# Reordering a causal linear attention with a top-2 mixture of experts behind it: low parts inside routing steps, q ahead of v, gathers moved up, gates read later, zeros written in other places

## The chip, the cores and the metric

One core of one Trainium2 chip runs the whole kernel. The metric is device time in microseconds of one execution, as the median of several runs. The profile is one further execution, and all rows below are from it.

## What is computed

The attention is a linear one with a decay per head: a state of 64 x 64 per head is decayed and added to at every step, and y is q times the state. Its output, 3072 tokens of 512 numbers, is x for the experts. Each token goes to the two of eight experts with the largest noisy logits.

```python
# q, k, v: (4, 8, 768, 64)
for t in range(S):
    state = gamma[None, :, None, None] * state + np.einsum('bhd,bhe->bhde', k[:, :, t], v[:, :, t])
    y[:, :, t] = scale * np.einsum('bhd,bhde->bhe', q[:, :, t], state)
x = y.transpose(0, 2, 1, 3).reshape(3072, 512)
logits = x @ w_gate
noisy_logits = logits + np.log1p(np.exp(x @ w_noise)) * noise
top2 = np.argpartition(-noisy_logits, 2, axis=1)[:, :2]
...
for e in range(8):
    for k in range(2):
        mask = top2[:, k] == e
        h = np.maximum(x[mask] @ w1[e], 0.0)      # 512 -> 1024
        out[mask] += top2_w[mask, k, None] * (h @ w2[e])
```

## The kernel before

Nothing is ordered by a scheduler: the order in which the Python code calls the helpers is the order of each engine's instructions, and tile pools add the waits. The kernel has three parts.

**The loop over 24 chunks** (4 batches of 6 chunks of 128 tokens, from 10 to 118.6 us). Chunk j of the loop runs, in this order: `qk(j+1)` on TensorE (q times k), `v_scale(j+1)` and `q_scale(j+2)` on GpSimd (decay tables into v and q, lines 339 and 345), the loads of chunk j+4 on SyncE's queue, `masked(j+1)` on VectorE (line 373), `x_store(j-3)`, `y_in(j)` on TensorE (line 379), then `x_total`, `x_hi` of chunk j-1 (sum of squares, power of two, high half of x in fp16 by ScalarE), then what the table `between` holds for chunk j, `y_mm(j)`, `x_rows(j-2)` (transposes), `logits(j-2)`, then what `todo` holds, then `slip()`, then what `late` holds. `slip()` runs `x_lo` of chunk j-1 on VectorE (line 417): the low half of x, what the fp16 high half leaves over. It is the last reader of that chunk's y in PSUM; there are two such buffers, so `y_in(j)` waits for `x_lo(j-2)`.

Routing of a batch is spread over the following chunks. With n the last chunk of batch b: `route_a` late in n+2 (logits, softplus), `route_b` between n+3 (top two: six `max`, six `max_index`), `route_b2` and `route_c` between n+4 (one-hot rows, `den` = second minus first logit at line 493, and three small rows `cb`), `places` on TensorE and `route_d` in n+5, `route_e` in n+6 and n+7 (one-hot tables), `route_w` in n+8 (gate weights, written to `gbuf`), `table` on TensorE at the end of n+8, `route_f` between n+9 (adds the table to `acc`). For the second batch, `rows_of` follows there (lines 596 to 599: row numbers `idx` for the gathers), then at the end of that chunk, 20, three indirect gathers `xg<-xbuf,idx` on GpSimd's queue (line 684), and in chunks 21 and 22 three DMA transposes `xe<-xg` on SyncE's queue (line 706): the input of the first expert. In chunks 11 to 19 GpSimd also makes the halves of the first expert's w1 (`wst`, `w1l`, lines 227 and 231).

SyncE's queue also carries the zeros that `out` starts from (the experts add into it): `zero_out(i)`, line 305, at the end of chunks 12, 14, 16, 18, 20 and 21, each two pieces of 512 KB in rows of 1 KB (one for either half of the columns), and in chunk 22 two of 128 KB.

**Between the loop and the second expert** (to about 195 us) TensorE runs the first expert for the batches that are routed, in small units (`early`: `mm1` for a first product, `mm2` for a second), between the last batch's routing steps. `mm1(0, SECOND, CAPS[0], n)`, n from 0 to 7, is the first expert's third part; in it stand `out_scale(0, mid, NBLK)` (gates of the rows, lines 952 to 961, from gathers `gx`) at n = 5 and, from n = 4, `x_sums(1)`: sums and differences of the second expert's transposed input on VectorE (lines 845 to 852), each with a ScalarE step `xt` (line 853).

**Experts 1 to 7** (`mm1s`, a Strassen-like first product of 30 slots, each six matmuls, with a `hook` after every slot; then `mm2`). At slot 11 the hook runs `out_scale(e, ...)`, which waits for the gathered gates `gx`.

## Time and profile before

| | us |
|---|---|
| median of 3 runs | 642.06 |
| lowest, highest of them | 640.72, 649.16 |
| the profiled execution | 644.05 |
| its span from first to last instruction | 642.3 |
| TensorE busy | 615.4 |
| VectorE busy | 451.6 |
| ScalarE busy | 392.3 |
| GpSimd busy | 394.0 |

The profile calls the engines PE (TensorE), PEld (its weight loads), DVE (VectorE), ACT (ScalarE), POOL (GpSimd) and SP (SyncE); SPq is SyncE's queue, which issues DMAs. A row of a timeline starts with the start in us from the span's start and the duration in us; in square brackets stands how long the engine was idle before it and what ended that. In a row of waits, the engine and its line stand left of the arrow, the one waited for right of it. A window's row gives each engine's busy time and number of instructions, then the granted TensorE clock, the busy share of the DMA engines and GB/s. Busy time of an engine says little on its own: a wait of TensorE moves the end, an idle VectorE does not.

### The profile page before, as it was taken

What the parts mean: (1) busy time and instruction counts of PE and PEld (TensorE: products, weight loads), DVE (VectorE), ACT (ScalarE), POOL (GpSimd) and SP (SyncE); (2) the same over time, 40 slices, a digit from 0 to 9 for tenths busy, and PEclk for the clock granted to TensorE, in tenths of its full rate; (3) what the DMA queues carried; (4) which work ended last, traced back from release to release, by engine and by line L of the source; (5) the groups of instructions that cost most, each with busy time, mean ns of one, the idle gap of its engine ahead of it and who ended that gap; (6) DMA issues with size and microseconds to landing.
All of it is one profiled execution on the core that took longest, in us unless ns stands there. A gap on an engine that the chain in (4) does not pass through costs nothing.

```text
span 642.3 us, 13225 instructions
## 1 busy us (share of the span) xinstructions
PE 615.4 (96%) x5133; PEld 387.0 (60%) x5133; DVE 451.6 (70%) x947; ACT 392.3 (61%) x655; POOL 394.0 (61%) x279
## 2 busy tenths in 40 slices
PE   8999988899989899999999999999999999999995
PEld 5898877656756444654465446544654465445784
DVE  4668999577768599179917991799279747957730
ACT  4688878763447656486648664866476558656311
POOL 3455998244477847882688457744883676484164
PEclk9999999999999899999999999999999999999998
DMA  8999999953966499459644974597469746942043
GB/s 307 340 391 404 383 381 336 289 193 103 179 105 166 77 155 308 53 110 206 211 52 82 205 243 52 93 194 245 51 103 193 230 48 112 243 53 33 7 53 44
DMA packets 107393, 112.90 MB, mean 176 GB/s; under 512 B 64512, under 2 KB 84224, under 8 KB 103744
## 3 DMA queue, kind: packets, MB, share of 16 engines
q1 hardware_dynamic: 86080, 84.29, 45.2%
q0 software_dynamic: 20528, 26.90, 27.1%
q8 instruction: 41, 0.67, 0.4%
q10 hardware_dynamic: 720, 0.84, 0.4%
q14 instruction: 24, 0.20, 0.1%
HBM read 72.16 MB, written 26.47 MB: 154 GB/s over the span
## 4 chain that ended last, share of the span: by engine, by line
PE 71%; DVE 11%; DMA 10%; ACT 3%; POOL 2%; issue 2%; SPq 0%; POOLq 0%; DVEq 0%; ACTq 0%
PE pO L997 10%; PE pO L998 10%; PE pO L996 10%; PE pH L895 9%; PE pH L896 9%; PE pH L897 9%; DMA xe<-xg 3%; DVE am L373 2%; DMA out<-ot,idx 2%; DMA in_k<-kT 2%; PE pO L987 1%; PE pO L986 1%; PE pO L985 1%; PE pA L366 1%; POOL out L972 1%
## 5 line engine op out<-in xcount | busy, mean ns | idle before, releaser
L972 POOL DMA_INDIRECT out<-ot,idx x108 | 194.3, 1799 | 143.7 <-ACT ot L966 57.8
L996 PE MATMUL pO<-w2h,h 128*128 128x512 f16 x336 | 127.5, 379 | 1.7 <-ACT h L822 1.7
L998 PE MATMUL pO<-w2h,h 128*128 128x512 f16 x336 | 127.5, 380 | 0.0
L997 PE MATMUL pO<-w2l,h 128*128 128x512 f16 x336 | 127.5, 379 | 0.0
L919 DVE TENSOR_TENSOR s<-pH,s 128x416 f32<-128x416 f32 (+2 forms) x84 | 47.3, 572 | 46.3 <-PE pH L897 38.3
L694 POOL DMA_INDIRECT gx<-gbuf,idx x54 | 61.0, 1129 | 28.1 <-issue 13.3
L684 POOL DMA_INDIRECT xg<-xbuf,idx x55 | 58.5, 1063 | 26.6 <-issue 14.3
L966 ACT ACTIVATE ot<-pO,gse 128x512 f32<-128x512 f32 (+2 forms) x48 | 32.6, 682 | 59.9 <-PE pO L998 56.2
L190 ACT ACTIVATE junk<-wst 128x1024 bf16<-128x1024 f32 x64 | 67.8, 1059 | 0.0
L915 ACT ACTIVATE s<-pH 128x416 f32<-128x416 f32 (+2 forms) x84 | 40.3, 507 | 33.3 <-PE pH L897 33.3
L895 PE MATMUL pH<-xt,wsh 128*128 128x416 f16 (+2 forms) x168 | 56.8, 338 | 2.8 <-DVE h L912 2.8
L911 ACT ACTIVATE h<-s 128x832 f16<-128x832 f32 (+2 forms) x42 | 35.9, 871 | 35.7 <-DVE s L919 35.7
L996 PEld LDWEIGHTS <-h 128*128 128x128 f16 x336 | 32.9, 98 | 40.7 <-ACT h L822 2.0
L998 PEld LDWEIGHTS <-h 128*128 128x128 f16 x336 | 32.9, 98 | 40.0 <-DVE h L823 0.6
L896 PE MATMUL pH<-xt,wsh 128*128 128x416 f16 (+2 forms) x168 | 56.7, 338 | 0.0
L897 PE MATMUL pH<-xt,wsl 128*128 128x416 f16 (+2 forms) x168 | 56.7, 338 | 0.0
L997 PEld LDWEIGHTS <-h 128*128 128x128 f16 x336 | 32.9, 98 | 38.8
L219 DVE SCALAR_TENSOR_TENSOR w2l<-wst,wsc,w2h 128x1024 f16<-128x1024 f32 x28 | 35.8, 1280 | 14.1 <-ACT w2h L214 14.1
L339 POOL TENSOR_TENSOR vp<-in_v,ct 128x512 f32<-128x512 f32 x24 | 25.1, 1046 | 31.5 <-issue 14.6
L853 ACT ACTIVATE xt<-s 128x832 f16<-128x832 f32 (+2 forms) x28 | 24.5, 874 | 30.8 <-DVE s L852 30.5
L912 DVE SCALAR_TENSOR_TENSOR h<-s,h 128x832 f16<-128x832 f32 (+2 forms) x42 | 41.0, 991 | 2.6 <-ACT h L911 2.6
L373 DVE TENSOR_TENSOR am<-pA,ct 128x512 f32<-128x512 f32 x48 | 30.8, 682 | 11.1 <-PE pA L366 11.1
(216 smaller groups left out, 1491.5 us busy)
## 6 DMA issues: line engine op xcount, KB each, us to landing
wst<-w SPq DMA_DIRECT2D x28, 1024.0 KB, 7.8
in_q<-qT SPq DMA_DIRECT2D x24, 256.0 KB, 5.8
in_k<-kT SPq DMA_DIRECT2D x24, 256.0 KB, 5.4
in_v<-vt SPq DMA_DIRECT2D x24, 256.0 KB, 5.6
xbuf<-xr SPq DMA_DIRECT2D x24, 256.0 KB, 6.0
out<-zero SPq DMA_DIRECT2D x12, 512.0 KB, 6.8
in_kt<-kt SPq DMA_DIRECT2D x20, 256.0 KB, 5.5
wst<-w SPq DMA_DIRECT2D x8, 512.0 KB, 6.5
```

The lines of the kernel that those rows point to most:

```text
L190: nc.scalar.activation(junk, st[:, i * 1024:(i + 1) * 1024], AF.Square, accum_out=ss[:, i:i + 1])
L373: nc.vector.tensor_tensor(AM[j][:, s], pA[s], mask[:, None, :].to_broadcast([128, HP, C]), op=OP.mult)
L684: nc.gpsimd.indirect_dma_start(out=x[:p1], out_offset=None, in_=xbuf[:128 + rows], in_offset=bass.IndirectOffsetOnAxis(ap=idx[:p1, i:i + 1 ...
L694: nc.gpsimd.indirect_dma_start(out=GX[e][:, t, :], out_offset=None, in_=gbuf[:128 + rows], in_offset=bass.IndirectOffsetOnAxis(ap=idx[:, i ...
L895: nc.tensor.matmul(p, wh, bh[:, k, :], start=start and k == 0, stop=False, skip_group_check=True)
L896: nc.tensor.matmul(p, wh, bl[:, k, :], start=False, stop=False, skip_group_check=True)
L897: nc.tensor.matmul(p, wl, bh[:, k, :], start=False, stop=(k == 1), skip_group_check=True)
L919: nc.vector.tensor_tensor(s[:, u], p, s[:, u], op=OP.add)
L972: nc.gpsimd.indirect_dma_start(out=out[s], out_offset=bass.IndirectOffsetOnAxis(ap=idx[:n, i:i + 1], axis=0), in_=ot[:n, s * HD:(s + 1) * ...
L996: nc.tensor.matmul(p, a, WT["2h"][:, f, :], start=(f == 0), stop=False)
L997: nc.tensor.matmul(p, a, WT["2l"][:, f, :], start=False, stop=False)
L998: nc.tensor.matmul(p, c, WT["2h"][:, f, :], start=False, stop=(f == FT - 1))
```

## The change

1. `slip()` (x's low part) is called inside `route_b` (after the six `max`), inside `route_b2` (after `den`) and inside `route_w`, and at the end of a chunk ahead of `todo`. `den` takes one operand from a copy in PSUM (`second_best`).
2. `places` is called ahead of `x_total`. The casts and copies of constants move from chunks 1 and 2 to the ends of chunks 3 to 5.
3. On GpSimd `q_scale(j+2)` stands ahead of `v_scale(j+1)`; v has three buffers in place of two; q of chunk 2 is scaled on VectorE.
4. `route_f` and `rows_of` move from between n+9 to the end of n+8; the three first gathers are issued in the middle of chunk 20, all three transposes at the end of chunk 21.
5. The far part of the table of constants and the noise are loaded on SyncE's queue (after chunk 2's q and k, and in chunk 3) in place of ScalarE's.
6. The zeros: one piece of 512 KB (in rows of 2 KB) at the end of each of the chunks 7 and 11 to 17, the two small ones in chunk 10, and four pieces behind the loop, ahead of `gates(0, 3, ...)`.
7. Behind the loop: `out_scale(0, mid, NBLK)` runs after the third part's `mm1`, `x_sums(1)` starts at n = 6, and the second expert's gates are read at slot 22 in place of 11.

```diff
+    second_best = pR[:, 256:256 + NC]
...
+    nc.sync.dma_start(ct[:, near:], ctab[:, near:])
...
     def zero_out(i):
...
+        o, i = out[i % 2], i // 2
         if i < 6:
-            for o in out:
-                nc.sync.dma_start(o[128 + i * 512:128 + (i + 1) * 512, :].rearrange("(p r) d -> p r d", p=128),
-                                  zero[:, None, :HD].to_broadcast([128, 4, HD]))
+            nc.sync.dma_start(o[128 + i * 512:128 + (i + 1) * 512, :].rearrange("(p a r) d -> p a (r d)", p=128, a=2),
+                              zero[:, None, :].to_broadcast([128, 2, DM]))
         else:
-            for o in out:
-                nc.sync.dma_start(o[:128, :], zero[:, :HD])
+            nc.sync.dma_start(o[:128, :], zero[:, :HD])
...
     def v_scale(j):
...
-        VP[j] = loads.tile([128, H, D], F32, name="vp", bufs=2)
+        VP[j] = loads.tile([128, H, D], F32, name="vp", bufs=3)
...
     def q_scale(j):
...
-        eng = nc.vector if j < 2 else nc.gpsimd
+        eng = nc.vector if j < 3 else nc.gpsimd
...
-    nc.scalar.dma_start(ct[:, near:], ctab[:, near:])
-    nc.scalar.dma_start(nz.rearrange("p c e -> p (c e)"), noise)
...
         for c in range(NC):
             nc.vector.max(m8[:, c, :], ny[:, c, :])
+        slip()
         for c in range(NC):
             nc.vector.max_index(i8[:, c, :], m8[:, c, :], ny[:, c, :])
...
         nc.vector.tensor_tensor(mb, wide, oh[:, 0], op=OP.add)
         den = work.tile([128, NC], F32, name="den", bufs=B)
-        nc.vector.tensor_tensor(den, m8[:, :, 1], m8[:, :, 0], op=OP.subtract)
+        nc.vector.tensor_copy(second_best, m8[:, :, 1])
+        nc.vector.tensor_tensor(den, second_best, m8[:, :, 0], op=OP.subtract)
+        slip()
...
         nc.vector.reciprocal(dn, small[:, 12:12 + NC])
+        slip()
...
         nc.vector.tensor_tensor(g[:, 0], invp[b % 2], dn, op=OP.mult)
         nc.vector.tensor_tensor(g[:, 1], g[:, 0], den, op=OP.mult)
...
-    between, late = {}, {}
+    between, late, ahead_of = {}, {}, {}
     for b in range(B - 1):
         n = (b + 1) * NC - 1
         late.setdefault(n + 2, []).append((route_a, (b,)))
...
-        steps = [(3, route_b, b), (4, route_b2, b), (4, route_c, b), (5, places, b), (5, route_d, b),
+        steps = [(3, route_b, b), (4, route_b2, b), (4, route_c, b), (5, route_d, b),
                  (6, route_e, b, 0), (7, route_e, b, 1), (8, route_w, b)]
         if b == B - 2:
             steps = steps[:-2]
         else:
             at(n + 8, table, b)
-            between.setdefault(n + 9, []).append((route_f, b))
+            late.setdefault(n + 8, []).append((route_f, (b,)))
         if b == B0 - 1:
...
-            between[n + 9] += [(rows_of, acc, 0, 3)]
+            late[n + 8].append((rows_of, (acc, 0, 3)))
             for t in range(3):
-                at(n + 9, gather, 0, t, 0, 128, B0 * S)
-            between.setdefault(n + 10, []).append((x_t, 0, 0))
-            at(n + 10, x_t, 0, 1)
-            between.setdefault(n + 11, []).append((x_t, 0, 2))
+                ahead_of.setdefault(n + 9, []).append((gather, 0, t, 0, 128, B0 * S))
+                at(n + 10, x_t, 0, t)
+        ahead_of.setdefault(n + 5, []).append((places, b))
         for s in steps:
             between.setdefault(n + s[0], []).append(s[1:])
     at(0, gate_sum)
-    at(1, nc.vector.tensor_copy, trib, K("tri"))
+    at(3, nc.sync.dma_start, nz.rearrange("p c e -> p (c e)"), noise)
+    late.setdefault(4, []).append((nc.vector.tensor_copy, (trib, K("tri"))))
...
-    for i in range(7):
-        at((12, 14, 16, 18, 20, 21, 22)[i], zero_out, i)
-    at(2, nc.vector.tensor_copy, lanes16, K("lanes"))
-    at(2, nc.vector.tensor_copy, blks16, K("blks"))
-    at(2, nc.vector.tensor_copy, lanes.bitcast(F32), lanes16.bitcast(F32))
-    at(2, nc.vector.tensor_copy, blks.bitcast(F32), blks16.bitcast(F32))
-    at(2, nc.vector.tensor_copy, lidx[0], K("lidx"))
-    at(2, nc.vector.tensor_copy, lidx[1], K("lidx3"))
+    for i in range(8):
+        at((7, 11, 12, 13, 14, 15, 16, 17)[i], zero_out, i)
+    for i in range(2):
+        at(10, zero_out, 12 + i)
+    for j, a in ((4, (lanes16, K("lanes"))), (4, (blks16, K("blks"))), (5, (lanes.bitcast(F32), lanes16.bitcast(F32))),
+                 (5, (blks.bitcast(F32), blks16.bitcast(F32))), (5, (lidx[0], K("lidx"))), (5, (lidx[1], K("lidx3")))):
+        late.setdefault(j, []).append((nc.vector.tensor_copy, a))
...
             y_in(0)
         if j + 1 < NCH:
             qk(j + 1)
-            v_scale(j + 1)
         if j + 2 < NCH:
             q_scale(j + 2)
+        if j + 1 < NCH:
+            v_scale(j + 1)
         if j + AHEAD < NCH:
...
         if j + 1 < NCH:
...
         if j:
             y_in(j)
+            for f, *a in ahead_of.get(j, []):
+                f(*a)
             x_total(j - 1)
...
         if j >= 2:
...
+        slip()
         for f, a in todo.get(j, []):
             f(*a)
-        slip()
         for f, a in late.get(j, []):
             f(*a)
...
     route_a(b)
     early(1)
     route_b(b)
-    early(1)
     route_b2(b)
     route_c(b)
+    early(1)
...
     w_sum(1, "1", 0)
     early(1)
...
     w_sum(1, "1", 1)
     early(1)
     route_w(b - 1)
+    for i in range(8, 12):
+        zero_out(i)
     gates(0, 3, (B - 1) * S)
     route_e(b, 0)
     out_scale(0, 0, 3)
...
-        if n == 5:
-            out_scale(0, mid, NBLK)
...
-        if n == 4:
+        if n == 6:
             xs1 = x_sums(1)
-        if n > 3:
+        if n > 5:
             xs1(1)
...
         if n == 0:
+            out_scale(0, mid, NBLK)
...
-            xs1(4)
+            xs1(5)
...
         if n == 1:
-            xs1(1)
+            xs1(2)
...
-            if s == 11:
+            if s == (22 if e == 1 else 11):
                 out_scale(e, 0, len(blocks(e)))
```

What moved is told best by the engines' orders. First VectorE in the routing step of the third batch, chunk 21 (`oh`, `mb`: one-hot rows; `m`: the eight largest logits; `x`: the low part; `am`: the mask of the chunk after). Before:

```order
L491 TENSOR_TENSOR mb<-pR,oh 128x60
L493 TENSOR_TENSOR den<-m_2064 128x6
L513 TENSOR_SCALAR cb<-pR 128x10
L514 TENSOR_TENSOR cb<-pR,ct 128x10
L515 COPY cb<-pR 128x10
L417 SCALAR_TENSOR_TENSOR x_2160<-pY,upx,x_2160 128x512
L373 TENSOR_TENSOR am<-pA,ct 128x512 x2
```

and now:

```order
L491 TENSOR_TENSOR mb<-pR,oh 128x60
L493 COPY pR<-m_2075 128x6
L494 TENSOR_TENSOR den<-pR,m_2075 128x6
L416 SCALAR_TENSOR_TENSOR x_2162<-pY,upx,x_2162 128x512
L515 TENSOR_SCALAR cb<-pR 128x10
L516 TENSOR_TENSOR cb<-pR,ct 128x10
L517 COPY cb<-pR 128x10
```

The low part stands three rows earlier, and `den` has one operand in SBUF where it had two. Next GpSimd at the end of the loop, from the last half of w1 to the row with chunk 23's v. Before:

```order
L231 TENSOR_TENSOR w1l<-wst_502,w1h 128x2x512
L339 TENSOR_TENSOR vp<-in_v,ct 128x512
L345 TENSOR_TENSOR qs<-in_q,gq 128x512
L684 DMA xg<-xbuf,idx 128x1024 x3
L339 TENSOR_TENSOR vp<-in_v,ct 128x512
L345 TENSOR_TENSOR qs<-in_q,gq 128x512
L339 TENSOR_TENSOR vp<-in_v,ct 128x512
```

and now:

```order
L232 TENSOR_TENSOR w1l<-wst_496,w1h 128x2x512
L346 TENSOR_TENSOR qs<-in_q,gq 128x512
L340 TENSOR_TENSOR vp<-in_v,ct 128x512
L687 DMA xg<-xbuf,idx 128x1024 x3
L346 TENSOR_TENSOR qs<-in_q,gq 128x512
L340 TENSOR_TENSOR vp<-in_v,ct 128x512 x2
```

Each q has changed places with a v; the three gathers still stand between chunk 22's q and chunk 23's. Last, VectorE in the second expert's first product (`s`, `h`: sums and halves of h; `w2l`: a half of w2; `gm`, `gsm`, `gse`: the gates). Before:

```order
L919 TENSOR_TENSOR s<-pH,s 128x416
L912 SCALAR_TENSOR_TENSOR h_2385<-s,h_2385 128x2x416
L952 TENSOR_TENSOR i_3547<-wsc_2318,wsc_2526 128x1
L959 TENSOR_TENSOR gm<-gx,onef 128x7
L960 TENSOR_REDUCE gsm<-gm 128x7
L961 TENSOR_SCALAR gse<-gsm,i_3547 128x7
L912 SCALAR_TENSOR_TENSOR h_2385<-s,h_2385 128x2x416
L219 SCALAR_TENSOR_TENSOR w2l<-wst_2524,wsc_2526,w2h 128x1024
L912 SCALAR_TENSOR_TENSOR h_2385<-pH,h_2385 128x416
```

and now:

```order
L917 SCALAR_TENSOR_TENSOR h_2384<-s,h_2384 128x2x416 x2
L220 SCALAR_TENSOR_TENSOR w2l<-wst_2523,wsc_2525,w2h 128x1024
L917 SCALAR_TENSOR_TENSOR h_2384<-pH,h_2384 128x416
L924 TENSOR_TENSOR s<-pH,s 128x416
L917 SCALAR_TENSOR_TENSOR h_2384<-pH,h_2384 128x416
L924 TENSOR_TENSOR s<-pH,s 128x416 x2
L957 TENSOR_TENSOR i_3645<-wsc_2319,wsc_2525 128x1
L964 TENSOR_TENSOR gm<-gx,onef 128x7
L965 TENSOR_REDUCE gsm<-gm 128x7
L966 TENSOR_SCALAR gse<-gsm,i_3645 128x7
```

The four rows of the gates stand seven instructions later, behind the second `h` that TensorE needs there.

## Rows read from the trace of the kernel before

**Rows 1.** The page, part 1: busy time, share of the span and instructions of each engine.

```profile
PE 615.4 (96%) x5133; PEld 387.0 (60%) x5133; DVE 451.6 (70%) x947; ACT 392.3 (61%) x655; POOL 394.0 (61%) x279
```

**Rows 2.** Waits of TensorE, whole span: us in total, times, longest us.

```profile
PE pY L379 <- DVE x L417: 5.8, 6, 2.0
PE pA L366 <- POOL qs L345: 3.3, 4, 1.7
PE pH L895 <- DVE h L912: 2.8, 1, 2.8
PE pH L819 <- DMA xe<-xg: 2.5, 1, 2.5
PE pO L996 <- ACT h L822: 1.7, 1, 1.7
```

**Rows 3.** Timeline of TensorE: start us, us, instruction [idle before <- what ended it].

```profile
13.62 1.53 PE L366 MATMUL pA<-qs,in_k 64*128 64x128 f32 x16 [1.72 <-POOL qs L345]
...
103.78 1.16 PE L366 MATMUL pA<-qs,in_k 64*128 64x128 f32 x16
106.18 1.09 PE L379 MATMUL pY<-am,vp 128*64 128x128 f32 x16 [1.24 <-DVE x L417]
...
110.07 1.16 PE L366 MATMUL pA<-qs,in_k 64*128 64x128 f32 x16 [0.67 <-POOL qs L345]
111.99 1.09 PE L379 MATMUL pY<-am,vp 128*64 128x128 f32 x16 [0.75 <-DVE x L417]
...
121.13 0.32 PE L819 MATMUL pH<-xe,w1h 128*128 128x384 f16 x1 [2.53 <-DMA xe<-xg]
```

**Rows 4.** Timeline of VectorE, in the routing steps of three batches.

```profile
79.20 3.25 DVE L493 TENSOR_TENSOR den<-m 128x6 f32<-128x6 f32 x1
...
98.47 0.16 DVE L523 TENSOR_SCALAR pR<-den 128x6 f32<-128x6 f32 x1
...
130.81 1.13 DVE L596 TENSOR_SCALAR padv<-acc,ct 128x2 f32<-128x2 f32 x1
...
138.23 0.16 DVE L493 TENSOR_TENSOR den<-m 128x6 f32<-128x6 f32 x1
```

**Rows 5.** Windows: stretch; us; five engines' busy (instructions); clock; DMA share; GB/s.

```profile
37.00:66.00 29.00, 27.88 (x533) 26.09 (x531) 22.84 (x92) 24.48 (x49) 16.39 (x14) 1.00 1.04 405
66.00:101.00 35.00, 31.62 (x603) 29.34 (x601) 32.91 (x122) 28.47 (x59) 33.50 (x23) 1.00 1.06 380
140.00:160.00 20.00, 20.00 (x134) 11.39 (x132) 16.18 (x53) 9.75 (x17) 7.02 (x6) 1.00 0.49 148
219.10:222.50 3.40, 3.40 (x11) 1.41 (x11) 0.89 (x2) 0.52 (x1) 2.71 (x3) 0.50 0.46 86
```

**Rows 6.** Timeline of SyncE's queue: chunk 22's load of q.

```profile
92.06 0.38 SPq L277 DMA_DIRECT2D in_q<-qT  x1
```

**Rows 7.** The tile in_q (loads of q), all 24 loads.

```profile
DMA to landing us min/median/max: 4.0/5.8/7.0
```

**Rows 8.** Timeline of GpSimd around the first gathers.

```profile
98.37 2.15 POOL L231 TENSOR_TENSOR w1l<-wst,w1h 128x1024 f16<-128x1024 f32 x1
...
101.45 1.31 POOL L345 TENSOR_TENSOR qs<-in_q,gq 128x512 f32<-128x512 f32 x1
104.02 1.19 POOL L684 DMA_INDIRECT xg<-xbuf,idx  x1 [1.25 <-DMA xbuf<-xr]
...
107.75 1.05 POOL L339 TENSOR_TENSOR vp<-in_v,ct 128x512 f32<-128x512 f32 x1
108.75 1.27 POOL L345 TENSOR_TENSOR qs<-in_q,gq 128x512 f32<-128x512 f32 x1
```

**Rows 9.** Timelines of ScalarE and VectorE behind the loop.

```profile
185.71 0.90 ACT L853 ACTIVATE xt<-s 128x832 f16<-128x832 f32 x1 [4.85 <-DVE s L852]
...
215.74 0.17 DVE L959 TENSOR_TENSOR gm<-gx,onef 128x7 f32<-128x7 f32 x1 [3.42 <-DMA gx<-gbuf,idx]
```

## The prediction, written before the changed kernel ran

> **What bounds the kernel now.** I read the page's first part, then the waits of TensorE, then its timeline at the longest waits, then the windows, and only then the engines that it waits for. TensorE is busy for 615.4 of 642.3 us [rows 1], so 26.9 us are all that any reordering can touch. Five kinds of wait make 16.1 us of them [rows 2]: on x's low part (5.8, six times), on the scaled q (3.3, four times), on one VectorE step of the second expert (2.8), on the first transposed gather (2.5), on one h of the first expert (1.7). A wait can also cost afterwards: behind the 2.8 us one the granted clock is 0.50, the lower of the two levels, from 219.1 to 222.5 [rows 5], and 3.4 us at half speed are 1.7 us lost. The windows show what stands right behind TensorE inside the loop. The DMA share is 1.04 at 405 GB/s from 37 to 66 us and 1.06 at 380 GB/s from 66 to 101 us: the transfers have no room left. And GpSimd is busy for 33.5 of the 35 us from 66 to 101 [rows 5].
>
> **The routing steps.** The subtraction `den` takes 3.25 us where GpSimd is at work beside it, and 0.16 us where it is not [rows 4]. x's low part stands behind it on VectorE, and the next y waits for that. The change copies one operand to PSUM first and moves the low part ahead of the three `cb` rows, and in the other step ahead of six index searches. If the copy runs free, copy and `den` are 2 x 0.16 us; if it is held as `den` was, 3.25 + 0.16 us. I take 0.16, by the nearest row: at 98.47 VectorE reads `den` in SBUF and writes PSUM in 0.16 us [rows 4], in the middle of GpSimd's w1l, which runs from 98.37 for 2.15 us [rows 8]. Then the 5.8 us go as local waits. The Trainium skill (VectorE: DVE Perf Modes, "Why PSUM operands drop a tier") says that an operand in PSUM keeps an operation out of the modes that use both read ports, which would leave the copy alone; no row here shows such a copy beside GpSimd.
>
> **q ahead of v.** On GpSimd a q takes 1.27 us and a v 1.05 [rows 8]. The three q waits inside the loop are 3.3 - 1.72 = 1.6 us together, the last 0.67 [rows 2, 3], each below the 1.05 us by which q comes earlier: gone. The 1.72 us at 13.62 is the wait for chunk 2's q; that scaling goes to VectorE, but ahead of the mask of chunk 1, so between 0 and 1.7 us are won (and the table's far half no longer loads beside it). I need no value for it, for this reason:
>
> **What stays: the loads set the pace.** Take the load of q for chunk 22. SyncE issues it at 92.06 [rows 6]; at the median of 5.8 us [rows 7] it lands at 97.9. With 1.27 us of scaling it could serve TensorE at 99.1; TensorE takes it at 103.78 [rows 3], so it is 4.6 us early. Ahead of that load the old order has 6 of the 512 KB pieces of zeros (chunks 12, 14, 16), the new one 8 and two small ones, together 8.5 pieces. A piece is 0.524 MB: 1.38 us at the 380 GB/s of the stretch with 1 KB rows, 1.29 us at 405 GB/s, which I take for the new 2 KB rows. So 8.5 x 1.29 = 11.0 against 6 x 1.38 = 8.3: the load lands 2.7 us later, and q is ready at 99.1 + 2.7 = 101.8. Of the waits ahead of this point (5.8 - 1.24 - 0.75 for x and 1.6 - 0.67 for q, 4.7 us, plus the start) only 103.78 - 101.8 = 2.0 us can arrive. The bounds are 2.0 (transfers full throughout) and 4.7 (a load never late).
>
> **The first gathers.** They stay behind q22 and v21 on GpSimd, but their row numbers are made a chunk's end earlier. From q22 ready at 101.8: v21 1.05, then the three gathers, which with the gaps take 107.75 - 104.02 = 3.73 [rows 8], then q23 1.27: 107.9, against 110.07 before [rows 3]. So 2.2 us arrive here, and behind it the wait of 0.75 goes. The loop's last matmul, at 121.13 - 2.53 = 118.6 before, ends at 118.6 - 2.2 - 0.75 = 115.7. Is the transposed input there? Before it took 121.13 - 104.02 = 17.1 us from the first gather, with four pieces of zeros (chunks 20 and 21) in its way, 4 x 1.38 = 5.5 us; now 102.9 + 17.1 - 5.5 = 114.5. Just early enough, and the 2.53 us go as well. The loop is worth 121.13 - 115.7 = 5.4 us.
>
> **Behind the loop.** Four pieces of zeros, 4 x 1.29 = 5.2 us of transfers, come ahead of the transposes of the first expert's third part. From 140 to 160 us the DMA share is 0.49 [rows 5], some 10 us free. If they fit there they cost nothing, if they stand in front of the transposes up to 5.2; I take 0.5. The half of x's sums that stood at n = 4 goes to n = 6 and after: its ACT step waited 4.85 us for VectorE at 185.71 [rows 9] and the h for which TensorE waited 1.7 us came behind it on ScalarE. Now h is ahead of it: 1.7 us go. VectorE's sums end later by at most the 2.6 us of two units, while two whole rows of mm2 stand between; late sums are a rival below. The gates of the second expert were read at slot 11, where VectorE stood 3.42 us for the gather, until 215.74 [rows 9]; TensorE's 2.8 us followed. At slot 22, eleven products later, the gather has long landed, so the 2.8 us and the 1.7 us of clock go. Together 1.7 + 2.8 + 1.7 - 0.5 = 5.7 us.
>
> **Sum.** 5.4 + 5.7 = 11.1 us off the profiled execution's 644.05 us gives 632.9. The median of the runs, 642.06, lies 2.0 below that execution, so the forecast is 631.0 us. What a measurement of this kernel can tell from no change is about 2%: below 629.2 is faster, above 654.9 slower.
>
> **The rivals.**
> - The loads don't set the pace: larger packets and the later pieces leave enough room. Then all of 4.7 and the 0.75 arrive, and so does some of the start. For it: the load was 4.6 us early. Against it: a DMA share of 1.04 and more for 64 us [rows 5]. The loop would win up to 9.9 us (5.8 + 1.6 + 2.53) in place of 5.4: 626.5. Chance 0.18.
> - The row numbers of the first gathers meet GpSimd. Before, the gathers waited for them, so GpSimd had nothing to do between its q of 101.45 and 104.02 [rows 8]; now the steps come at the end of the chunk before, while GpSimd still has w1l, q22 and v21 to do, and the first of them once took 1.13 us, at 130.81 [rows 4]. VectorE could stand there for 2.15 + 1.27 + 1.05 = 4.5 us, with the mask and x's low part behind it. Some of that is covered: chunk 21 needs 110.07 - 103.78 - 1.24 - 0.67 = 4.4 us of TensorE, which from 101.8 would be at 106.2, and waits for q23 until 107.9 anyway. So 4.5 - 1.7 = 2.8 us are lost, and the loop wins 2.6 in place of 5.4: 633.8. Chance 0.17. Here a rule speaks against the change: the Trainium skill (SBUF — State Buffer, "Who interferes with whom") says that a VectorE instruction with two SBUF inputs is blocked while a GpSimd instruction reads SBUF. The 3.25 us of `den` agree. By that rule two of the moved steps are held, and 633.8 would be the time.
> - The second expert's wait comes back, since VectorE's sums now lie two units later: 2.8 + 1.7 are not won: 635.5. Chance 0.08.
> - The copy to PSUM is held as `den` was, so the change does not do what it says: the routing waits stay, the loop wins 2.53 and 0.7: 633.2. Chance 0.03.
> - Slower: the clock. The 2.8 us at 219, and perhaps the 1.72 at 13.62, are of a size after which it can fall. If the late loads make TensorE wait that long before each of the eight chunks 14 to 21, and each wait is followed by 3.4 us at 0.50 as at 219.1, that is 8 x 1.7 = 13.6 us: 644.6. It decides once the waits are some 1.7 us each; against it, TensorE was idle for 3.4 of the 35 us from 66 to 101 and was granted 1.00 throughout [rows 5]. Chance 0.04.
>
> **How the numbers follow.** The forecast has 0.50 and its own range 628.5 to 633.5. The rivals at 633.2, 633.8 and 635.5 stretch the upper end, with the four pieces' full 5.2 us in part: 637. The rival at 626.5, with some of the start, sets the lower end: 625.5. Left out are the clock and the far ends, under 2 in 10. Below 629.2 lie most of the first rival (0.15) and a quarter of the forecast (0.13): 0.28 faster. Slower than 654.9 needs the clock rival and more: 0.02. The rest, 0.70, is within 2%.
>
> **What would show it.** Right: `den` at 0.16 us in all four batches; no TensorE wait on x's low part above 0.5 us; in the windows a DMA share of 1.0 still up to 100 us and TensorE's waits in chunks 14 to 22 on q (GpSimd or its load) instead; no wait before the first matmul on xe; no wait near 187 and 219, and the clock at 1.00 there. Wrong: no q waits in the loop (then 626), or VectorE's row-number steps at 1 us and more before chunk 21 (then 634), or a new wait of TensorE on xe near 165 us, which would be the zeros.

## The result, and the profile after

| | before | after |
|---|---|---|
| median of 6 runs, us | 643.07 | 635.85 |
| lowest, highest, us | 640.72, 649.16 | 632.04, 637.60 |
| the profiled execution, us | 644.05 | 632.04 |
| its span, us | 642.3 | 630.3 |

The ratio of the runs is 0.987, with a 95% interval of 0.9821 to 0.9919: faster by 1.3%, clear of no change but within the 2% that the forecast set as its bound. The forecast was 631.0 us, 625.5 to 637.0. The time lies in the range, 4.9 us above the forecast; 7.2 us came off where 11.1 were forecast.

One thing has to be seen before any profile is read: the profiled execution is also the fastest of the six. Read alone, it says that the forecast for it (632.9) was 0.9 us off and all is well. The other five took 634.92 to 637.60.

The page's busy time and the waits of TensorE after, against [rows 1, 2]; the waits' columns are us in total, times, longest:

```profile
PE 611.6 (97%) x5133; PEld 384.9 (61%) x5133; DVE 451.2 (72%) x952; ACT 391.8 (62%) x655; POOL 395.2 (63%) x278
```

```profile
PE pA L365 <- POOL qs L346: 3.9, 6, 1.2
PE pL L407 <- DVE lg L458: 1.9, 1, 1.9
...
PE pY L378 <- DVE x L416: 0.8, 2, 0.4
```

The waits on x's low part fell from 5.8 to 0.8 us, the one on xe from 2.5 to 0.7, and the two behind the loop, 2.8 and 1.7 us, are no longer listed. The waits on q grew from 3.3 to 3.9, and one is new: 1.9 us at a matmul that sums squares, put down to `lg`, the next batch's logits on VectorE. TensorE's timeline gives its place:

```profile
15.88 1.16 PE L365 MATMUL pA<-qs,in_k 64*128 64x128 f32 x16
...
100.86 0.19 PE L407 MATMUL pL<-xss,oneb 128*64 128x1 bf16 x2 [1.91 <-DVE lg L458]
...
107.65 1.16 PE L365 MATMUL pA<-qs,in_k 64*128 64x128 f32 x16
...
115.74 0.32 PE L824 MATMUL pH<-xe,w1h 128*128 128x384 f16 x1 [0.69 <-DMA xe<-xg]
```

Chunk 3's q times k starts at 15.88 us (19.06 before). In the kernel before, the clock was low there, behind the wait of 1.72 us for chunk 2's q; its window reads

```profile
15.00:18.00 3.00, 3.00 (x34) 2.89 (x34) 1.87 (x6) 0.50 (x1) 1.83 (x2) 0.55 0.97 305
```

and after the change the clock is 1.00 at the start of the loop. The first matmul on xe starts at 115.74, 5.4 us earlier than in [rows 3]. VectorE in front of 100.86, with `den` of the third batch below:

```profile
97.22 2.60 DVE L599 TENSOR_SCALAR padv<-acc,ct 128x3 f32<-128x3 f32 x1
99.74 0.15 DVE L600 TENSOR_SCALAR neg<-acc 128x3 f32<-128x3 f32 x1
99.92 0.16 DVE L601 TENSOR_TENSOR neg<-neg,padv 128x3 f32<-128x3 f32 x1
100.12 0.16 DVE L602 SCALAR_TENSOR_TENSOR idx<-acc,neg 128x3 int32<-128x3 f32 x1
...
107.12 0.17 DVE L493 COPY pR<-m 128x6 f32<-128x6 f32 x1
107.32 0.16 DVE L494 TENSOR_TENSOR den<-pR,m 128x6 f32<-128x6 f32 x1
```

The first of the four steps that make the row numbers `idx` takes 2.60 us. It ends as GpSimd's w1l ends:

```profile
81.00 1.26 POOL L346 TENSOR_TENSOR qs<-in_q,gq 128x512 f32<-128x512 f32 x1 [3.23 <-DMA in_q<-qT]
...
97.66 2.14 POOL L232 TENSOR_TENSOR w1l<-wst,w1h 128x1024 f16<-128x1024 f32 x1
100.13 1.29 POOL L346 TENSOR_TENSOR qs<-in_q,gq 128x512 f32<-128x512 f32 x1 [0.33 <-DMA in_q<-qT]
101.38 1.04 POOL L340 TENSOR_TENSOR vp<-in_v,ct 128x512 f32<-128x512 f32 x1
102.59 1.18 POOL L687 DMA_INDIRECT xg<-xbuf,idx  x1 [0.17 <-DVE p2m L167]
...
106.31 1.28 POOL L346 TENSOR_TENSOR qs<-in_q,gq 128x512 f32<-128x512 f32 x1
```

GpSimd has no gap from 81.00 to 99.80, waits 0.33 us for the load of chunk 22's q, and issues the first gather at 102.59, right behind v: by then the row numbers are ready. Behind the gathers it ends chunk 23's q at 107.59, and TensorE takes it at 107.65, with no wait: the 1.9 us of the hold end just where TensorE would have had to wait for this q in any case. Two windows of [rows 5] read now

```profile
66.00:101.00 35.00, 29.23 (x559) 26.75 (x556) 29.85 (x117) 26.26 (x53) 30.24 (x21) 1.00 1.06 373
219.10:222.50 3.40, 3.40 (x18) 1.53 (x16) 3.13 (x7) 2.99 (x3) 2.79 (x3) 1.00 1.03 164
```

so the transfers are still full to 101 us, and the clock at 219 us is 1.00.

### The profile page after: what moved, and what is told of

The parts are those of the page before. It is cut to its first block, busy times and chain, and to the rows that moved or that the text cites. A ratio compares the mean times of both kernels' runs of the same rounds, so it can differ in the third digit from the quotient of the medians.

```text
span 630.3 us, 13242 instructions
## 1 busy us (share of the span) xinstructions
PE 611.6 (97%) x5133; PEld 384.9 (61%) x5133; DVE 451.2 (72%) x952; ACT 391.8 (62%) x655; POOL 395.2 (63%) x278
## 4 chain that ended last, share of the span: by engine, by line
PE 83%; DVE 8%; DMA 3%; ACT 2%; issue 1%; POOL 1%; SPq 1%; POOLq 0%; ACTq 0%; DVEq 0%
PE pO L1001 11%; PE pO L1002 11%; PE pO L1003 11%; PE pH L900 11%; PE pH L902 10%; PE pH L901 10%; PE pA L365 2%; DVE am L372 2%; PE pY L378 2%; PE pO L992 2%; PE pT L1016 2%; PE pO L990 1%; PE pO L991 1%; PE pH L824 1%; DMA in_q<-qT 1%; PE pH L826 1%
## 5 line engine op out<-in xcount | busy, mean ns | idle before, releaser
L901 PE MATMUL pH<-xt,wsh 128*128 128x416 f16 (+2 forms) x168 | 56.0, 333 | 0.0
L900 PE MATMUL pH<-xt,wsh 128*128 128x416 f16 (+2 forms) x168 | 56.0, 333 | 0.0
L346 POOL TENSOR_TENSOR qs<-in_q,gq 128x512 f32<-128x512 f32 x21 | 26.7, 1273 | 26.3 <-DMA in_q<-qT 17.2
L900 PE MATMUL pH<-xe,w1h 128*128 128x416 f16 (+2 forms) x112 | 37.3, 333 | 0.1
```

The source lines that it names most:

```text
L900: nc.tensor.matmul(p, wh, bh[:, k, :], start=start and k == 0, stop=False, skip_group_check=True)
L901: nc.tensor.matmul(p, wh, bl[:, k, :], start=False, stop=False, skip_group_check=True)
```

## The experiments

Twelve kernels ran in three groups, each group on one chip together with the kernel before. The chips differ: its median was 653.06 us in group 1, 646.64 in group 2, 652.16 in group 3. Times and ratios are therefore compared inside a group only. On the chip of group 1 the changed kernel alone is not clear of no change (e1 in the table); the 1.3% of the result and f1's 1.6% were measured apart from it.

| kernel | group | median, us | ratio to before (95%) |
|---|---|---|---|
| e1_again (nothing edited) | 1 | 649.21 | 0.9964 (0.9927 to 1.0001) |
| e2_no_loop_zeros | 1 | 645.17 | 0.9872 (0.982 to 0.9924) |
| e3_rows_free | 1 | 650.84 | 0.9943 (0.9904 to 0.9983) |
| e4_routing_undone | 1 | 649.15 | 0.9948 (0.9917 to 0.998) |
| f1_control (nothing edited) | 2 | 635.73 | 0.9836 (0.9797 to 0.9876) |
| f2_behind_undone | 2 | 641.85 | 0.9958 (0.9925 to 0.9991) |
| f3_rows_psum | 2 | 634.20 | 0.9802 (0.9766 to 0.9839) |
| f4_zeros_late | 2 | 634.22 | 0.9809 (0.977 to 0.9847) |
| g0_rows_psum (as f3) | 3 | 646.95 | 0.9943 (0.99 to 0.9985) |
| g1_gates_late | 3 | 645.72 | 0.9905 (0.9866 to 0.9944) |
| g2_gates_zeros_late | 3 | 643.40 | 0.9892 (0.9846 to 0.9938) |
| g3_gathers_undone | 3 | 648.38 | 0.9945 (0.9917 to 0.9972) |

**The changed kernel twice more: e1_again and f1_control.** What was expected:

> The changed kernel once more, nothing edited, with another profile. Its profiled execution took 632.0 us with a mean granted clock of 0.996, its five timed runs 634.9 to 637.6 with 0.992 or 0.993. Theory A, a clock drop that comes in some executions only: the profile of a run near 635 shows a stretch at 0.50 that the first one did not have, some 3.4 us long (1.7 us lost), behind a short wait of TensorE. Theory B, the difference is nothing but scatter over the whole span: a profile near 635 shows the same clock and longer waits everywhere, none over 0.5 us more than in the first.

> The changed kernel, nothing edited, as the measure for the others of this call. In its two profiles so far the wait behind the row numbers was 1.9 us with the clock at 1.00 behind it and 3.9 us with a stretch at 0.50 behind it. Theory A (the wait's length varies with how VectorE's steps fall between GpSimd's, and the clock falls behind the longer ones): another wait of 2 to 4 us stands there, and the granted clock falls if it is nearer to 4. Theory B (the first profile is the rule): 1.9 us and no fall.

f1's profiled execution took 635.1 us, about its median, so it is taken for the usual run; the first profile was not taken in its group. VectorE at the row numbers:

```profile
98.07 0.45 DVE L599 TENSOR_SCALAR padv<-acc,ct 128x3 f32<-128x3 f32 x1
98.44 2.17 DVE L600 TENSOR_SCALAR neg<-acc 128x3 f32<-128x3 f32 x1
100.64 1.18 DVE L601 TENSOR_TENSOR neg<-neg,padv 128x3 f32<-128x3 f32 x1
101.85 0.97 DVE L602 SCALAR_TENSOR_TENSOR idx<-acc,neg 128x3 int32<-128x3 f32 x1
```

and GpSimd beside it:

```profile
97.44 1.06 POOL L340 TENSOR_TENSOR vp<-in_v,ct 128x512 f32<-128x512 f32 x1
98.44 2.14 POOL L232 TENSOR_TENSOR w1l<-wst,w1h 128x1024 f16<-128x1024 f32 x1
100.52 1.27 POOL L346 TENSOR_TENSOR qs<-in_q,gq 128x512 f32<-128x512 f32 x1
101.75 1.05 POOL L340 TENSOR_TENSOR vp<-in_v,ct 128x512 f32<-128x512 f32 x1
...
106.84 1.28 POOL L346 TENSOR_TENSOR qs<-in_q,gq 128x512 f32<-128x512 f32 x1
```

The first four end at 98.50, 100.58, 101.79 and 102.80, and VectorE's four steps at 98.52, 100.61, 101.82 and 102.82: each step ends as the GpSimd instruction beside it does, and the next step meets the next instruction. In the first profile the first step was held and the other three slipped through behind it, 3.1 us together; here it is 4.8. TensorE's wait:

```profile
103.39 0.22 PE L407 MATMUL pL<-xss,oneb 128*64 128x1 bf16 x2 [3.66 <-DVE lg L458]
...
111.45 1.16 PE L365 MATMUL pA<-qs,in_k 64*128 64x128 f32 x16
...
118.71 0.32 PE L824 MATMUL pH<-xe,w1h 128*128 128x384 f16 x1
```

It is 3.66 us in place of 1.91, and behind it the clock is at the lower of its two levels (the column before the last two is the granted clock):

```profile
103.40:106.80 3.40, 3.40 (x40) 3.28 (x41) 3.32 (x18) 2.06 (x7) 2.80 (x3) 0.50 0.96 203
106.80:110.00 3.20, 3.20 (x61) 3.05 (x60) 2.31 (x17) 2.39 (x4) 3.17 (x4) 1.00 0.91 245
```

The 3.4 us at 0.50 cost 1.7 us more. The first matmul on xe starts at 118.71, 3.0 us later than in the first profile; from there to the last matmul's end it is 507.1 us in both. So the difference between the two profiles lies in the loop, and most of it at this one place (0.8 us was there before: chunk 21's q times k starts at 97.55 in f1, at 96.76 in the first profile). Here the hold is no longer hidden: chunk 23's q is ready at 108.12, and TensorE takes it at 111.45, 3.3 us later. Theory A for f1. The same wait is 2.65 us in f2, 3.57 in e2, 3.69 in e4 and 3.86 in e1, which all keep these four steps, so the first profile's 1.91 is the shortest of six. The five other runs of the result have a mean granted clock of 0.992 or 0.993, against 0.996 in the profile, and 3.4 us at 0.50 lower the mean over 630 us by 0.003: that fits a fall in each of them, but no trace shows it. In e1 a stretch at 0.50 follows the wait as well, and another one a wait of 2.28 us on q at 84 us, as theory A has it, but that chip adds something of its own: VectorE and ScalarE show idle times put down to "issue" (8.5 and 13.4 us over the span, against 0 in the first profile and in f1), in places that differ from run to run. The profile shows no cause for them; the kernel before is 10 us slower there too.

**No zeros in the loop: e2.** Edit:

```diff
-    for i in range(8):
-        at((7, 11, 12, 13, 14, 15, 16, 17)[i], zero_out, i)
-    for i in range(2):
-        at(10, zero_out, 12 + i)
```

> The changed kernel without the ten writes of zeros inside the loop (those rows of the output are not set to zero; the four pieces behind the loop stay). Theory A, the loads set the pace (the forecast): the waits of TensorE on q, 3.9 us, fall under 1 us, GpSimd's wait of 3.2 us for the load of q at 81 us is gone, the loop ends 2 us or more earlier, and the time is 2 to 4 us below the changed kernel. Theory B, GpSimd sets the pace, since from 81 to 99.8 us it works without a break: the waits on q stay at 2.5 to 4 us, and the time is within 1 us of the changed kernel.

TensorE has no wait on q left in its list; the wait behind the row numbers stays:

```profile
PE pL L407 <- DVE lg L458: 3.6, 1, 3.6
```

The median is 4.0 us below e1's, and the ratios, 0.9872 and 0.9964, have intervals that do not overlap (though its profiled execution, 649.97, is its slowest run). The first matmul on xe starts at 118.22, 4.3 us before e1's 122.47. Theory A: the transfers set the pace of the chunks from 13 on, not GpSimd's own work, though GpSimd is busy for 33.9 of the 35 us from 66 to 101 there.

**The routing steps undone: e4.** Edit (and no `slip()` in `route_b` and `route_w`, and `slip()` behind `todo` at a chunk's end):

```diff
-        nc.vector.tensor_copy(second_best, m8[:, :, 1])
-        nc.vector.tensor_tensor(den, second_best, m8[:, :, 0], op=OP.subtract)
-        slip()
+        nc.vector.tensor_tensor(den, m8[:, :, 1], m8[:, :, 0], op=OP.subtract)
```

> The changed kernel with the routing steps as before: x's low part behind the index searches, behind den and the cb rows, no copy to PSUM, and the low part behind the other work at the end of a chunk. Both theories: den takes 1.5 to 3.3 us again where GpSimd works, and the waits on x's low part come to 4 us or more. Theory A (the forecast: q and the loads take most of this back anyway): the loop's end moves by 2 us or less and the waits on q shrink by what the others grow. Theory B (every local wait is paid): the time is 4 to 5 us above the changed kernel.

The time is e1's, 649.15 against 649.21 us, as theory A has it. But what both theories expected did not come, so this is a weak test: the waits on x's low part are 2.1 us and not 4, since `den` is hardly held:

```profile
50.01 0.16 DVE L492 TENSOR_TENSOR den<-m 128x6 f32<-128x6 f32 x1
...
76.33 0.89 DVE L492 TENSOR_TENSOR den<-m 128x6 f32<-128x6 f32 x1
...
110.72 0.16 DVE L492 TENSOR_TENSOR den<-m 128x6 f32<-128x6 f32 x1
```

0.16 us twice and 0.89 once, where the kernel before had 0.16, 3.25 and 2.81. With q and v exchanged, GpSimd's long instructions stand elsewhere. How long a step is held is a matter of what happens to run beside it, and what the copy to PSUM saves in the new order is not shown by e4.

**The row numbers freed: e3 and f3.** e3 copies the counts to PSUM for the first step; f3 also keeps one intermediate there:

```diff
+        src = tk[:, n0:n1]
+        if n0 == 0:
+            nc.vector.tensor_copy(pR[:, 264:264 + n1], src)
+            src = pR[:, 264:264 + n1]
-        nc.vector.tensor_scalar(padv[:, n0:n1], tk[:, n0:n1], 0.0, K("pad"), op0=OP.is_equal, op1=OP.mult)
+        nc.vector.tensor_scalar(padv[:, n0:n1], src, 0.0, K("pad"), op0=OP.is_equal, op1=OP.mult)
```

```diff
+        if n0 == 0:
+            src, neg = pR[:, 264:264 + n1], pR[:, 268:268 + n1]
+            padv = padv[:, :n1]
+            nc.vector.tensor_copy(src, tk[:, :n1])
+            nc.vector.tensor_scalar(padv, src, 0.0, K("pad"), op0=OP.is_equal, op1=OP.mult)
+            nc.vector.tensor_scalar(neg, src, 0.0, float(TOK), op0=OP.is_lt, op1=OP.mult)
+            nc.vector.tensor_tensor(neg, neg, padv, op=OP.add)
+            nc.vector.scalar_tensor_tensor(idx[:, :n1], tk[:, :n1], 127.0, neg, op0=OP.add, op1=OP.add)
+            return
```

> The changed kernel with the row counts copied to PSUM ahead of the first gathers' row numbers, so that the step that took 2.60 us beside GpSimd has one operand in SBUF less. Both theories: that step falls to some 0.2 us and the wait of 1.9 us at 100.9 goes. Theory A (the rival that the row numbers meet GpSimd, priced in full): 1.9 us come off the time. Theory B (it was hidden): the transposes of the first gathers, which end at 115.6 us whatever the row numbers do since GpSimd stands at q and v until 102.4, set the end of the loop; the wait on xe grows from 0.7 to about 2.5 us and the time stays within 0.5 us.

> The changed kernel with the four steps of the first gathers' row numbers arranged so that each reads or writes PSUM (counts and one intermediate there, one step more). Both theories: no step takes over 0.25 us, the wait in front of the sums of chunk 20 falls below 0.3 us, and the clock does not fall there. Theory A (the hold counts, and with it the clock): the loop ends 3 us or more earlier than in the control and the time is 2 to 5 us lower. Theory B (the gathers, which stand behind q and v on GpSimd, and their transposes end the loop anyway): the wait on xe becomes 2 us or more and the time stays within 1 us of the control.

In e3 the freed step took 0.22 us, and the hold went on to the next ones:

```profile
99.05 0.22 DVE L603 TENSOR_SCALAR padv<-pR,ct 128x3 f32<-128x3 f32 x1
99.18 0.18 DVE L604 TENSOR_SCALAR neg<-acc 128x3 f32<-128x3 f32 x1
99.39 2.04 DVE L605 TENSOR_TENSOR neg<-neg,padv 128x3 f32<-128x3 f32 x1
101.47 1.24 DVE L606 SCALAR_TENSOR_TENSOR idx<-acc,neg 128x3 int32<-128x3 f32 x1
```

The wait fell only from 3.9 us to 2.7, the clock fell behind it all the same, and the time, 650.84 us, is not below e1's: neither theory's case. In f3 no step is held, though w1l runs from 100.51 to 102.65 beside them:

```profile
100.40 0.17 DVE L602 COPY pR<-acc 128x3 f32<-128x3 f32 x1
100.60 0.22 DVE L603 TENSOR_SCALAR padv<-pR,ct 128x3 f32<-128x3 f32 x1
100.74 0.16 DVE L604 TENSOR_SCALAR pR<-pR 128x3 f32<-128x3 f32 x1
100.93 0.17 DVE L605 TENSOR_TENSOR pR<-pR,padv 128x3 f32<-128x3 f32 x1
101.14 0.16 DVE L606 SCALAR_TENSOR_TENSOR idx<-acc,pR 128x3 int32<-128x3 f32 x1
```

Still only 1.5 us came off (634.20 against 635.73, intervals overlapping), less than theory A's 2, and the wait on xe of theory B did not come: neither theory's number. What took its place is in TensorE's list and on GpSimd:

```profile
PE pA L365 <- POOL qs L346: 7.0, 7, 2.3
```

```profile
83.84 1.26 POOL L346 TENSOR_TENSOR qs<-in_q,gq 128x512 f32<-128x512 f32 x1 [4.79 <-DMA in_q<-qT]
```

The waits on q are 7.0 us, where f1 has 4.5, and the clock fell behind one of them, 2.3 us at 85. They follow a load of q that GpSimd waited 4.8 us for. One more, 1.85 us at 110.88, is the wait for chunk 23's q behind the gathers: the one in which the first profile's hold was hidden.

**The gates' write: f4, and group 3.** f4 takes four more pieces of zeros out of the loop; g1 writes the first batch's gates with the second's:

```diff
-    for i in range(8):
-        at((7, 11, 12, 13, 14, 15, 16, 17)[i], zero_out, i)
+    for i in range(4):
+        at((7, 11, 12, 13)[i], zero_out, i)
...
     x_store(NCH - 1)
+    for i in range(4, 8):
+        zero_out(i)
```

```diff
-        nc.sync.dma_start(gbuf[128 + b * S:128 + (b + 1) * S, :].rearrange("(c p) e -> p c e", p=128), gateb[:, sl])
+        if b:
+            a = 0 if b == 1 else b
+            nc.sync.dma_start(gbuf[128 + a * S:128 + (b + 1) * S, :].rearrange("(c p) e -> p c e", p=128),
+                              gateb[:, a * NC:(b + 1) * NC])
```

> As f3_rows_psum, and the four pieces of zeros of chunks 14 to 17 written behind the loop, ahead of the row numbers of the first expert's second part (eight pieces behind the loop in all). Theory A (the loads set the pace): GpSimd's waits for a load of q fall, the waits of TensorE on q between 82 and 97 us fall from 3 us to under 1.5, and the time is 1.5 to 4 us below f3_rows_psum. Theory B (GpSimd's own work sets it, or the pieces cost the same behind the loop): within 1 us of f3_rows_psum, or with a new wait on xe behind the loop.

> f3_rows_psum once more, as the measure for the next two. In its profile GpSimd waited 4.8 us for the load of q at 83.8 us, TensorE's waits on q were 7.0 us together, and the transfers, at 400 GB/s before and after, fell to 160 to 250 GB/s from 77 to 81 us, behind the write of the first batch's gates (768 packets of 40 bytes, issued at 73.5 us). The same low stretch is expected here.

> As g0, but the first batch's gates are written together with the second batch's, 28 us later, when the last loads are issued. Theory A (the write of small packets is what slows the transfers near 78 us, and with them the load of q): they stay above 330 GB/s from 74 to 84 us, GpSimd's wait for the load of q there falls from 4.8 to under 1.5 us, TensorE's waits on q from 7.0 to under 4, and the time is 1.5 to 4 us below g0; the low stretch near 104 us gets longer and may cost the transposes of the first expert 1 us. Theory B (the low stretch has another cause, the zeros beside it above all): it stays, and the time is within 1 us of g0.

> As g1, with the four pieces of zeros of chunks 14 to 17 behind the loop as in f4_zeros_late. Theory A (the loads set the pace of these chunks, and in f4 only the gates' write hid it): TensorE's waits on q fall below those of g1, under 2 us together, and the time is 0.5 to 2 us below g1. Theory B (GpSimd's own work sets what is left): the waits on q stay as in g1 and the time is within 0.5 us of g1 or above it.

In f4 nothing changed (634.22 against 634.20 us, theory B's number): GpSimd's wait for that load was 4.7 us, the waits on q 6.2. So the pieces of these chunks were not what made it late. In g1 most of it is gone (1.58 us; 3.51 in g0, on the same chip). The same four us in f3 and in g1 (the last column is GB/s):

```profile
77.00:81.00 4.00, 3.84 (x74) 3.36 (x70) 2.85 (x11) 1.72 (x5) 2.04 (x2) 1.00 1.10 210
```

```profile
77.00:81.00 4.00, 3.92 (x80) 3.51 (x76) 3.01 (x14) 3.79 (x10) 2.42 (x4) 1.00 1.05 400
```

```profile
79.76 1.27 POOL L346 TENSOR_TENSOR qs<-in_q,gq 128x512 f32<-128x512 f32 x1 [1.58 <-DMA in_q<-qT]
```

```profile
PE pA L365 <- POOL qs L346: 2.3, 4, 0.8
```

With a write of 30 KB in 768 packets in front, everything moves at 210 GB/s for 4 us (225 in g0), though the DMA engines count as fully busy; without it at 400. The write alone does not make TensorE wait: e2, without zeros in the loop, has it too (258 GB/s from 72 to 76 us), and no load is late there. The waits on q are 2.3 us (g0: 6.1), and the first matmul on xe starts at 117.28, 5.1 us before g0's 122.36 (g0's profile is its slowest run). Theory A for the mechanism. The time does not show it: 645.72 us against 646.95, and g2 643.40; 0.4% and 0.5% by the ratios, with overlapping intervals. In g1 the low stretch now stands from 101 to 110 us, and behind the loop this chip adds a wait of 2.8 us on an h. In g2 the waits on q are 4.4 us, not less than in g1: neither theory's number.

**Behind the loop undone: f2.** Edit (and `xs1(4)`, `xs1(1)` in the third part's `mm2`):

```diff
-        if n == 6:
+        if n == 4:
             xs1 = x_sums(1)
-        if n > 5:
+        if n > 3:
             xs1(1)
...
-            out_scale(0, mid, NBLK)
...
+        if n == 5:
+            out_scale(0, mid, NBLK)
...
-            if s == (22 if e == 1 else 11):
+            if s == 11:
```

> The changed kernel with the part behind the loop as before: gates of the second expert read at slot 11, x's sums from n = 4, the gates of the first expert's third part at n = 5. The four pieces of zeros behind the loop stay. Theory A (the forecast: 1.7 us of wait on an h of the first expert, 2.8 us at the second expert and 1.7 us of clock behind it): both waits come back, the clock falls to 0.50 behind the second, and the time is 5 to 6.5 us above the control. Theory B (those waits belonged to the timing of the old loop): they come back by less than half, and the time is at most 2.5 us above the control.

The median is 6.1 us above f1's: theory A by the time, though only one of its two waits came back. The wait on the gates and the clock behind it:

```profile
181.08 0.39 PE L1001 MATMUL pO<-w2h,h 128*128 128x512 f16 x1 [0.20 <-ACT h L827]
...
213.20 0.34 PE L900 MATMUL pH<-xt,wsh 128*128 128x416 f16 x1 [2.76 <-DVE h L917]
```

```profile
213.20:216.60 3.40, 3.40 (x12) 1.56 (x12) 0.95 (x2) 0.52 (x1) 2.77 (x3) 0.59 0.49 76
```

The 1.7 us on an h of the first expert (now at 181.08) came back as 0.2. From the first matmul on xe to the last one's end f2 has 512.1 us, f1 507.1, the kernel before 513.9: in the profile 5.0 us belong to the edits of f2, and 1.8 to the timing of what comes out of the loop.

**The gathers a chunk later: g3.** Edit, as in the kernel before:

```diff
-            late[n + 8].append((rows_of, (acc, 0, 3)))
+            between[n + 9] += [(rows_of, acc, 0, 3)]
             for t in range(3):
-                ahead_of.setdefault(n + 9, []).append((gather, 0, t, 0, 128, B0 * S))
-                at(n + 10, x_t, 0, t)
+                at(n + 9, gather, 0, t, 0, 128, B0 * S)
+            between.setdefault(n + 10, []).append((x_t, 0, 0))
+            at(n + 10, x_t, 0, 1)
+            between.setdefault(n + 11, []).append((x_t, 0, 2))
```

> The changed kernel with the row numbers, the three first gathers and their transposes where the kernel before has them (a chunk later). Theory A (the forecast: moving them is worth the 2.5 us wait on xe): the wait of 1.9 to 3.9 us in chunk 20 goes, a wait of 2 us or more on xe comes in its place, and the loop ends about where the changed kernel's does with the shorter hold (116 us) or later. Theory B (the move costs more than it brings, because the row numbers meet GpSimd there and the clock falls): the loop ends 1 us or more earlier than in the changed kernel's profile with the longer hold (118.7 us) and the time is 1 us or more below the changed kernel's, by its ratio to the kernel before.

Not settled. The row numbers were held there as well (steps of 1.38 and 1.09 us at 104.73), the wait of chunk 20 was replaced by one of 1.9 us in the next chunk, the wait on xe of theory A did not come, the profile (its slowest run) has a wait of 3.79 us on q at 77 us ahead of all this, and the ratio, 0.9945, cannot be told from e1's 0.9964, which is from another chip. Whether the move of the gathers pays by itself stays open.

## Why the prediction was right, and where its sum was not

**`den` and x's low part: right.** `den` took 0.16 us in all four batches and the copy 0.17 beside GpSimd's q. The forecast let only 2.0 of the 4.7 us of these waits arrive. How much did is not shown: e4 brought back 1.4 us of the waits on x's low part, at no cost in its time, and hardly any hold of `den`.

**The loads set the pace: right, and the reason half.** q of chunk 22 was ready at 101.42 us, forecast 101.8. TensorE's lead over the kernel before is 3.2 us at chunk 3's q times k and 4.9 at chunk 18's, and the waits on q bring it down to 2.6 at chunk 21's: the start needed no value, as the forecast said. e2 shows the pace directly. But the forecast worked it out from pieces of zeros alone. f4 and g1 show that the load near 80 us, for which GpSimd waits 3 to 5 us in most profiles, is late mainly because of 768 small packets, which the sum did not contain (and, by e2, not without zeros in the loop).

**The first gathers: the term that was too small.** "In the loop 5.4" rested on row numbers that cost nothing. In the first profile the loop did bring 5.4, along the forecast's own path: chunk 23's q was ready at 107.59 (forecast 107.9), and the 1.9 us of the hold cost nothing because TensorE would have waited for that q. That this execution drew a short hold was luck. In f1 the wait is 3.7 us and the clock takes 1.7 more, which is more than that q can hide, and the loop brings 121.13 - 118.71 = 2.4, 3.0 less than forecast. This is the rival that the row numbers meet GpSimd. Its 2.8 us are near the 3.0, but made up otherwise: it had 4.5 us of hold, 1.7 of them hidden, and no clock. (For f1's execution: 2.4 in the loop and 6.8 behind it from 644.05 give 634.9, and it took 635.1.) The forecast for the median also took the kernel before as 642.06, where six runs give 643.07. With 3.0 more for the loop, 1.1 less behind it and this 1.0, 631.0 becomes 633.9; the other 2 us to 635.85 are not accounted for. The rule of the Trainium skill named there (SBUF — State Buffer, "Who interferes with whom") agrees with what the runs show: one-input steps were held too (2.17 us in f1), and the section counts `tensor_scalar` among the operations that can take the shared ports, when their operands meet its conditions. With the row of 1.13 us [rows 4], that was reason for more than 0.17, and the prediction's own sign of being wrong, row-number steps at 1 us and more, came. f3 wins back only 1.5 us, with overlapping intervals, so without the hold 631.0 would probably not have been reached either: the load near 80 us is late there too.

**Behind the loop: right.** Forecast 5.7 us; 6.8 by the profiles, 6.1 by f2's median. The gates are the larger part; the 1.7 us on the h depended on the old loop's timing more than on x's sums, by f2's one profile. The four pieces of zeros, forecast at 0.5, show no wait: behind its first matmul on xe TensorE has no gap above 0.3 us in f1.

**The clock.** As a slower rival it was put at eight small falls; between TensorE's first matmul and its last the clock falls not at all in the first profile, once in f1, f3, g1 and g2, and two or three times in the other eight. Most falls stand behind a wait of 1.2 to 3.9 us, some behind waits of 0.7 us and less (110.7 us in e2), and not each wait has one (1.91 us in the first profile, 2.65 in f2 and 2.75 in g1 had none). The kernel before had two, behind the 1.72 us at the start and the 2.8 us at 219; the change removed both, and the forecast had only the second in its sum.

## What to carry to other kernels

One profile of a kernel with a hold between VectorE and GpSimd is one draw: the same four short steps cost 3.1 us in one run and 4.8 in another, by what ran beside them. Profile more than once, and see whether the profiled run is near the median. Before moving short VectorE steps beside long GpSimd instructions, give each of them a PSUM operand, not only the first; the hold passes on to the next. And a hold that fits into a wait which comes anyway costs nothing until it outgrows it: in the first profile 1.9 us cost nothing, in f1 the wait and the clock behind it, 5.4 us together, cost 3. A forecast should say how long a hold can become before it shows.

## What the runs showed of the hardware that was not expected

- A write of 768 packets of 40 bytes slows the transfers around it to 210 GB/s for 4 us (f3, 77 to 81 us) from 400 without it (g1), at a DMA share of 1.10 and 1.05; in e2, without zeros beside it, to 258 GB/s (72 to 76 us), with no load late. Why the kernel before lost less at the same write (342 GB/s from 75 to 79 us) was not found.
- Chains of short steps are held one GpSimd instruction each: 0.45, 2.17, 1.18 and 0.97 us in f1, where 0.2 us each is free.
- In groups 1 and 3 the kernel before takes 652 to 653 us, elsewhere 643 to 647. In e1's profile, from one of the slower chips, VectorE and ScalarE show 8.5 and 13.4 us of idle time that the profile ties to nothing.
